# Rows of two tokens: probabilities loaded in the layout of their use, reordered keys sent behind weight piece 3, state copied instead of zeroed, zeroing late

## The chip, the cores and the metric

One core of one Trainium2 chip runs the kernel. The metric is the device time of one execution in microseconds (us). Before the change seven runs lie between 300.64 and 303.35 us, with a median of 302.35 us.

## The reference

```python
f = sigmoid(f_logit)                       # q, k, v, f_logit: [B=4, H=8, S=768, D=48]
for t in range(S):
    state = f[:, :, t, :, None] * state + k_t (x) v_t      # state: [B, H, D, D]
    y[:, :, t] = q_t . state
x = y in rows of tokens                    # [B*S = 3072, H*D = 384]
p = domain_probs / (domain_probs.sum(-1) + 1e-9)           # [3072, E = 4]
out = sum over e of p[:, e] * (relu(x @ w1[e]) @ w2[e])    # w1: 384 x 1024, w2: 1024 x 384
```

A gated linear attention feeds four experts, whose outputs are added with normalised probabilities per token. Probabilities, weights and inputs come from memory as 32-bit numbers; the matrix products are in bf16.

## The kernel before

**Tiling.** The sequence is cut into C = 6 chunks of T = 128 tokens. A chunk has four batches of 8 heads, so its experts work on 4 x 128 = 512 tokens. For a chunk c the attention takes cumulated gates (`cs`, a product with a triangular matrix), exponentials of them, the products q and k with these, their transposes (`tp`), scores (`at`) with a triangular mask, the output `y`, its transpose `xt` into `xT`, and the update of the state (`kv`, `ev_kv`, `state`). The experts take `h` (L476, w1), `relu` (L487 on ScalarE, L485 on VectorE), `o` (L491, w2) and `ev_o` (L498, L500, L502), where the probability of the token is the scalar. VectorE does every `ev_o` with e > 0.

**Chunk 0** has a form of its own: a row holds two tokens, and a tile of 128 rows holds 64 rows of each of two batches. Its products `q` and `k` are in that layout. For its state update (`kv 0.g`, L414) the keys are needed in rows of one batch, so they are sent once more through DMA: `dma_kc` (L371) sends eight copies of 64 KB, from tile `qk` to tile `kc`, on SyncE's queue.

**Who sets the order.** All steps are entered into a planner (`Plan`) with costs, priorities, buffers taken and lags. It plays them through once, and what it gives out is a fixed order of instructions on each engine. SyncE (SP) issues the loads, `dma_kc`, the stores and the DMA transposes in one queue; GpSimd (POOL) issues the loads of v of chunk 0 and eleven weight pieces, which are cast on the way; ScalarE (ACT) issues three early loads. Weight pieces w0 to w3 are halves of w1 for experts 0 and 1, w4 and w5 are halves of w2 for expert 0, and then come whole matrices: w6 is w1 of expert 2, w7 is w2 of expert 1, w8 is w1 of expert 3, w9 is w2 of expert 2, w10 is w2 of expert 3. `after` adds a wait of one transfer for another (f of chunk 1 waits for w6, its second part for w8). Expert products of chunk 0 and steps of attention 1 lie interleaved on TensorE (PE), in the planner's order. PSUM has four buffers `ps_m` for the experts and four `ps_t` for attention. Matmuls on a tile `busy` (L814) fill TensorE ahead of the first expert product where the planner saw a hole.

**At the start** GpSimd builds masks, zeroes pads, then Sf (the 32-bit state, L182) and two tiles Sb (the bf16 state, L186), and only then issues v. VectorE makes `par`, `parb` (L167, a cast of 128 x 2 numbers), `Ui` (L170), `Us` (L173) and masks, among them `mask01` (L180), which attention from chunk 1 on uses.

**Probabilities** are loaded as 24 rows of 2 KB (L277), copied once into the order of two tokens (L283), and turned by eight 32-bit transposes on TensorE (L287, L289) into a `ps_m` buffer. Four VectorE steps (L292 to L295) make `pn` from it.

Of the kernel before, what the change touches and what calls it, by code (L numbers as in the profile page):

```python
# [8 lines left out]
FP32 = mybir.dt.float32  # L9
BF16 = mybir.dt.bfloat16  # L10
# [15 lines left out]
class Plan:  # L26
# [32 lines left out]
    def run(self):  # L59
        for o in self.ops:  # L60
            for k in o.frees:
                self.left[k] = self.left.get(k, 0) + 1
        for o in self.ops:
            if o.name.split(" ")[-1].startswith("0.") and set(o.costs) & {"ACT", "DVE"}:
                o.lag += 0.1
        left = sorted(self.ops, key=lambda o: o.prio)
        free_at = {e: 0.0 for o in left for e in o.costs}
        free_at.update({"DMA": 0.8, "DVE": 5.4, "POOL": 4.6, "ACT": 0.7, "PE": 2.0})
        freeing, done, now = [], [], 0.0
        while left:  # L70
# [33 lines left out]
def kernel(  # L104
# [11 lines left out]
    nc = tc.nc  # L116
# [62 lines left out]
    mask01 = const.tile([T, NP * T], FP32)  # L179
    nc.vector.tensor_copy(out=mask01.rearrange("s (i t) -> s i t", i=NP), in_=U.unsqueeze(1).broadcast_to([T, NP, T]))  # L180
    Sf = const.tile([MP, B, NP, D], FP32)
    nc.gpsimd.memset(Sf, 0.0)  # L182
    Sb = []
    for i in range(2):
        t = const.tile([MP, B, NP, 2 * D], BF16, name=f"sb{i}")
        nc.gpsimd.memset(t, 0.0)  # L186
        Sb.append(t)
    NR = B * C
    praw = const.tile([NR, T, E], FP32)
    ident32 = const.tile([NR, 32], FP32, name="ident32")[:, 0:NR]  # L190
    nc.vector.tensor_copy(out=ident32, in_=ident[0:NR, 0:NR])
    pn = const.tile([T, 2, E, NR], FP32)
    psm = const.tile([T, 2, NR], FP32, name="psm")
    v0 = [const.tile([T, H, 2, D], BF16, name=f"v0{g}") for g in range(2)]
# [8 lines left out]
    for nm, a in (("f", f_logit), ("q", q), ("k", k), ("v", v)):  # L203
# [9 lines left out]
        "cs": ([T, 512], FP32), "tp": ([128, 2, NP, T], BF16), "A": ([T, NP, T], FP32), "y": ([T, 512], FP32),  # L213
        "KV": ([T, 512], FP32), "xp": ([T, KD, T], BF16), "hp": ([128, NT], FP32), "op": ([128, 512], FP32), "pp": ([T, 2, E, NR], FP32),
        "y0": ([T, 512], FP32), "A0": ([T, NP, T], FP32),
    }

    def tl(kind, *key):

        if (kind, key) not in tiles:  # L220
            room = kind if kind in rooms else "ps_m" if kind in ("hp", "op", "pp", "y0", "A0") else "ps_t"
            slot = P.slot[(room, kind) + key if room.startswith("ps_") else (room,) + key]
            if room in ("gp", "qk", "e"):
                tiles[kind, key] = pads[room, slot]
            else:
                shape, dt = shapes[kind]
                pool = ps if room.startswith("ps_") else wk
                tiles[kind, key] = pool.tile(shape, dt, name=f"{room}{slot}")
        return tiles[kind, key]
# [45 lines left out]

    def load_p():
        nc.sync.dma_start(out=praw, in_=moe_domain_probs.rearrange("(r p) e -> r p e", p=T))  # L277

    def praw0():
        return tl("v", 0, 0)[0:NR].rearrange("t h d -> t (h d)")[:, 0:T * E]  # L280

    def p_by_j(eng):
        copy(eng, praw0().rearrange("r (j p e) -> r j p e", j=2, e=E), praw.rearrange("r (p j) e -> r j p e", j=2))  # L283

    def pe_pp():
        for e in range(E):
            nc.tensor.transpose(out=tl("pp")[:, 0, e], in_=praw[:, :, e], identity=ident32)  # L287
        for e in range(E):
            nc.tensor.transpose(out=tl("pp")[:, 1, e], in_=praw0()[:, e::E], identity=ident32)  # L289

    def probs():
        nc.vector.tensor_reduce(out=psm, in_=tl("pp").rearrange("p a e r -> p a r e"), axis=mybir.AxisListType.X, op=ALU.add)  # L292
        nc.vector.tensor_single_scalar(out=psm, in_=psm, scalar=1e-9, op=ALU.add)
        nc.vector.reciprocal(out=psm, in_=psm)
        nc.vector.tensor_tensor(out=pn, in0=tl("pp"), in1=psm.unsqueeze(2).broadcast_to([T, 2, E, NR]), op=ALU.mult)  # L295

# [71 lines left out]
    def dma_kc(n):  # L368
        k = tl("qk", 0, n)[:, 1].rearrange("(p b) h d -> b p (h d)", b=2)
        for b in range(2):  # L370
            nc.sync.dma_start(out=kc[n // 2][b * P2:(b + 1) * P2, n % 2].rearrange("p h d -> p (h d)"), in_=k[b])  # L371

# [77 lines left out]

    def ev_kv(c, b):
        KV = tl("KV", c, b)[:, 0:HD].rearrange("m (i r d) -> m i r d", r=2, d=D)
        for r in range(2):
            rows = slice(r * P2, r * P2 + D)
            nc.vector.tensor_tensor(out=Sf[rows, b], in0=Sf[rows, b], in1=KV[rows, :, r, :], op=ALU.add)  # L455

# [37 lines left out]
    def ev_o(c, e, nt, part, cols, eng):  # L494
        op, o = tl("op", c, e, nt, part)[:, cols], tl("o", c, nt)[:, cols]
        pe = pn[:, 0 if c else 1, e, nt * C + c:nt * C + c + 1]
        if e > 0:
# [69 lines left out]
    def attention0(slot):  # L567
# [3 lines left out]
        def on(f, *x):  # L571
            return lambda e: f(*x)
# [5 lines left out]
        for n in range(B):  # L578
# [13 lines left out]
                       takes=[("qk", 0, n)], frees=[("q", 0, g), ("e", 0, n)])  # L592
            kcd[n] = P.add(f"kc 0.{n}", {"DMA": 0.4}, on(dma_kc, n), -453 + n, deps=[km, wd[2, 1][0]], frees=[("qk", 0, n)], lag=2.0)
            tk = P.add(f"tpk 0.{n}", {"PE": 0.4}, on(pe_tp, 0, n, 1), s(4), deps=[km], takes=[pt_("tp")], frees=[("qk", 0, n)], lag=0.05)
# [18 lines left out]
        for g in range(2):  # L613
# [4 lines left out]
            for b in bs:  # L618
                ek = P.add(f"ev_kv 0.{b}", {"DVE": 0.74}, on(ev_kv, 0, b), s15 + 0.1, deps=[kv], frees=[("ps_t", "KV", 0, b)])
                kvdone[0, b] = P.add(f"state 0.{b}", {"POOL": 1.75}, on(state, 0, b), s15 + 0.2, deps=[ek])  # L620
# [3 lines left out]
    def attention(c, slot, gran):  # L624
# [51 lines left out]
        for b in range(B):  # L676
# [3 lines left out]
            at, vb = AT_[b], VB[b]  # L680
            eA = [P.add(f"ev_at{r} {c}.{b}", {"DVE": 0.7 if c else 0.62}, on(ev_at, r), s(7) + 0.1 + 0.1 * r, deps=[at],
                        takes=[("AT", c, b)], frees=[pt_("A", r)]) for r in range(2)]
# [48 lines left out]
    def add_o(c, e, nt, half):  # L731
# [9 lines left out]
        if half == 1 or by_cols:  # L741
            w = 0.36 if by_cols else 0.62
            ev = oev[c, e, nt] = P.add(f"ev_o {c}.{e}.{nt}.{part}", {"ACT": 0.58, "DVE": 0.56} if e == 0 else {"DVE": w},
                                       lambda g: ev_o(c, e, nt, part, cols, g), p - 1,
                                       deps=[m, oev.get((c, e - 1, nt)), pdone], takes=[("o", c, nt)], frees=[key])
            if e == E - 1:
                P.add(f"store {c}.{nt}.{part}", {"DMA": 0.6}, lambda _: store(c, nt, cols), p - 25, deps=[ev], frees=[("o", c, nt)])

    attention0(lambda n, s: -200 + 14 * (n // 2) + (n % 2) + s * 0.8)
    pl = P.add("ld p", {"DMA": 0.2}, lambda e: load_p(), -989.5, lag=3.0)  # L750
    pj = P.add("p by j", {"POOL": 0.8, "DVE": 0.6}, lambda e: p_by_j(e), -1.5, deps=[pl] + xdone[0, B - 1], takes=[("v", 0, 0)])
    pp = P.add("pp", {"PE": 0.6}, lambda e: pe_pp(), -1, deps=[pj], takes=[("ps_m", "pp")], lag=0.2, frees=[("v", 0, 0)])
    pdone = P.add("probs", {"DVE": 0.9}, lambda e: probs(), 4, deps=[pp] + xdone[0, B - 1], frees=[("ps_m", "pp")])
    ALL, LO, HI = list(range(B)), [0, 1], [2, 3]

# [93 lines left out]
```

## Time and profile before

| | |
|---|---|
| the profiled execution | 301.53 us |
| its span, first to last instruction | 299.8 us |
| granted TensorE clock | 1.000 |
| median of seven runs | 302.35 us |
| TensorE busy | 289.6 us, 97% of the span |
| VectorE, ScalarE, GpSimd busy | 134.0, 172.6, 107.9 us |
| DMA | 36.95 MB in 128974 packets, 118812 of them under 512 B |
| kc, issue to landing | 2.8 to 11.9 us, median 10.3 |
| weight pieces of 384 KB and of 768 KB, issue to landing | median 8.5 and 16.3 us |

All times are us from the span's start. "PEld" is the loading of weights into TensorE, "SPq" and "POOLq" are the queues in which SyncE and GpSimd issue. A row of the timeline gives start, duration, engine, line, operation, output and input, and in brackets the idle time before it with what ended it. A row of the waits gives the waiting engine and line, what it waited for, and the total, the number and the longest. The chain is followed back from the last instruction, so its rows show what set the end.

### The profile page before, as it was taken

The numbers are of one execution on the slowest core, as the hardware profiler recorded it, in microseconds if no ns is written. First come the engines' busy times: TensorE is split into PE (matmuls) and PEld (weight loads), VectorE is DVE, ScalarE is ACT, GpSimd is POOL, SyncE is SP. The second block draws the span as 40 slices with busy tenths as digits, with TensorE's granted clock in tenths as the row PEclk, the third lists the DMA queues.
The fourth block names the chain that finished last, engine by engine and source line by source line (L and its number), as shares of the span: only waits on it lengthen the run. The fifth ranks groups of instructions, "written<-read, shape, count | busy, mean of one in ns | idle before, by whom it ended". The sixth has DMA issues, their size and how long they took to land.

```text
span 299.8 us, 5811 instructions
## 1 busy us (share of the span) xinstructions
PE 289.6 (97%) x2261; PEld 173.8 (58%) x2261; DVE 134.0 (45%) x265; ACT 172.6 (58%) x323; POOL 107.9 (36%) x181
## 2 busy tenths in 40 slices
PE   5899979999999999999999999999999999999995
PEld 2668635567767776455555555555555555555553
DVE  8775115985754675027273353433442322201223
ACT  4875535765665676676477575554465544475440
POOL 8570005847388259124638553235220000000000
PEclk9999999999999999999999999999999999999999
DMA  7999999975979989999799932102331100200002
GB/s 199 213 199 208 205 198 227 191 131 121 192 157 199 183 156 180 230 209 178 133 177 205 194 64 35 28 0 61 95 85 37 26 0 28 77 1 2 0 0 105
DMA packets 128974, 36.95 MB, mean 123 GB/s; under 512 B 118812, under 2 KB 128156, under 8 KB 128948
## 3 DMA queue, kind: packets, MB, share of 16 engines
q1 hardware_dynamic: 118164, 29.29, 49.1%
q0 software_dynamic: 9200, 6.72, 15.3%
q10 hardware_dynamic: 1584, 0.59, 0.8%
q8 instruction: 17, 0.28, 0.4%
q14 instruction: 9, 0.07, 0.1%
HBM read 31.51 MB, written 4.72 MB: 121 GB/s over the span
## 4 chain that ended last, share of the span: by engine, by line
PE 82%; DMA 7%; SPq 3%; ACT 3%; POOL 2%; DVE 1%; issue 1%; POOLq 0%; ACTq 0%
PE ps_m L476 37%; PE ps_m L491 36%; DMA kc<-qk 4%; DMA f<-in_f_logit_dram 3%; PE ps_t L422 2%; SPq L260 2%; PE ps_t L442 1%; POOL qk L352 1%; PE ps_t L438 1%; SPq L374 1%; PE ps_t L310 1%; ACT ex L298 1%; PE ps_t L361 1%; ACT gp L305 1%; PE ps_t L448 1%
## 5 line engine op out<-in xcount | busy, mean ns | idle before, releaser
L476 PE MATMUL ps_m<-xT,w_sb 128*128 128x512 bf16 (+1 forms) x720 | 154.7, 337 | 0.1
L487 ACT ACTIVATE h<-ps_m 128x512 bf16<-128x512 f32 (+1 forms) x188 | 98.5, 527 | 96.5 <-PE ps_m L476 94.2
L491 PE MATMUL ps_m<-w_sb,h 128*128 128x384 bf16 (+1 forms) x776 | 153.8, 324 | 0.0
L491 PEld LDWEIGHTS <-h 128*128 128x128 bf16 x776 | 75.1, 98 | 58.7
L498 DVE SCALAR_TENSOR_TENSOR o<-ps_m,pn,o 128x384 f32<-128x384 f32 (+1 forms) x73 | 44.6, 611 | 107.0 <-PE ps_m L491 99.1
L476 PEld LDWEIGHTS <-w_sb 128*128 128x128 bf16 x720 | 67.8, 98 | 41.2 <-issue 0.3
L485 DVE TENSOR_SCALAR h<-ps_m 128x256 bf16<-128x256 f32 (+1 forms) x52 | 26.1, 510 | 22.2 <-PE ps_m L476 19.8
L462 POOL TENSOR_TENSOR Sf<-Sf,egs 48x192 f32<-48x192 f32 x40 | 21.1, 527 | 37.5 <-DVE Sf L455 35.6
L352 POOL TENSOR_TENSOR qk<-q,e 128x384 bf16<-128x384 f32 x18 | 21.4, 1194 | 27.9 <-ACT e L335 25.5
L335 ACT ACTIVATE e<-ps_t 128x384 f32<-128x384 f32 x48 | 26.7, 667 | 3.2 <-PE ps_t L310 2.1
L431 DVE TENSOR_TENSOR AT<-ps_t,mask 128x512 bf16<-128x512 f32 x40 | 25.0, 683 | 4.7 <-PE ps_t L422 4.7
L455 DVE TENSOR_TENSOR Sf<-Sf,ps_t 48x192 f32<-48x192 f32 x40 | 14.0, 350 | 13.1 <-PE ps_t L448 9.6
L246 POOL CAST vb<-v 128x384 bf16<-128x384 f32 x17 | 8.4, 501 | 31.7 <-issue 14.7
L352 POOL TENSOR_TENSOR qk<-k,e 128x384 bf16<-128x384 f32 x18 | 17.9, 1000 | 4.8 <-DMA k<-in_k_dram 4.6
L463 POOL CAST sb<-Sf 48x192 bf16<-48x192 f32 x40 | 14.1, 352 | 2.6
L500 ACT ACTIVATE o<-ps_m,pn 128x384 f32<-128x384 f32 x22 | 12.8, 581 | 2.8 <-PE ps_m L491 2.0
L298 ACT ACTIVATE ex<-f 128x768 f32<-128x768 f32 (+1 forms) x14 | 10.5, 749 | 5.0 <-DMA f<-in_f_logit_dram 5.0
L342 POOL DMA_DIRECT2D egs<-e x16 | 9.1, 567 | 7.5 <-ACT e L335 7.5
L244 ACT CAST yb<-ps_t 128x384 bf16<-128x384 f32 x17 | 8.1, 477 | 6.2 <-PE ps_t L442 6.2
L305 ACT ACTIVATE gp<-ex 128x768 bf16<-128x768 f32 (+1 forms) x14 | 10.5, 753 | 0.3
L442 PE MATMUL ps_t<-vb,AT 128*128 128x48 bf16 x160 | 10.0, 185 | 0.0
L269 POOL DMA_DIRECT2D w_sb<-in_moe_w_dram x11 | 8.8, 811 | 3.1 <-DMA k<-in_k_dram 2.6
(81 smaller groups left out, 141.0 us busy)
## 6 DMA issues: line engine op xcount, KB each, us to landing
w_sb<-in_moe_w_dram POOLq DMA_DIRECT2D x5, 768.0 KB, 16.3
k<-in_k_dram SPq DMA_DIRECT2D x10, 384.0 KB, 5.2
q<-in_q_dram SPq DMA_DIRECT2D x10, 384.0 KB, 5.2
v<-in_v_dram SPq DMA_DIRECT2D x10, 384.0 KB, 5.6
out_dram<-o SPq DMA_DIRECT2D x19, 192.0 KB, 2.1
f<-in_f_logit_dram SPq DMA_DIRECT2D x9, 384.0 KB, 5.8
w_sb<-in_moe_w_dram POOLq DMA_DIRECT2D x6, 384.0 KB, 8.5
f<-in_f_logit_dram SPq DMA_DIRECT2D x5, 192.0 KB, 5.1
```

The source lines that it names most:

```text
L298: nc.scalar.activation(out=tl("ex", c, b)[:, 0:n * H], in_=tl("f", c, b // 2)[:, hh(b, n), :], func=AF.Exp, scale=-1.0)
L335: nc.scalar.activation(out=o, in_=i, func=AF.Exp, scale=1.0 if j else -1.0)
L352: engines[eng].tensor_tensor(out=tl("qk", c, b)[:, j, :, 0:D].rearrange("t (i r) d -> t i r d", r=2), in0=tl("qk"[j], c, b // 2)[:, hh(b), ...
L431: nc.vector.tensor_tensor(out=tl("AT", c, b)[:, r].rearrange("s i t -> s (i t)"), in0=tl("A", c, b, r).rearrange("s i t -> s (i t)"), in1= ...
L455: nc.vector.tensor_tensor(out=Sf[rows, b], in0=Sf[rows, b], in1=KV[rows, :, r, :], op=ALU.add)
L462: nc.gpsimd.tensor_tensor(out=Sf[rows, b], in0=Sf[rows, b], in1=eg, op=ALU.mult)
L463: nc.gpsimd.tensor_copy(out=nb[rows, b, :, r * D:(r + 1) * D], in_=Sf[rows, b])
L476: nc.tensor.matmul(out=hp(c, e, fc, n0, n1, nf)[:, f], lhsT=w1_sb[:, e, kk, (fc + f) * 128:(fc + f + 1) * 128], rhs=tl("xT", c)[:, kk, n0: ...
L485: nc.vector.tensor_relu(out=dst, in_=src)
L487: nc.scalar.activation(out=dst, in_=src, func=AF.Relu)
L491: nc.tensor.matmul(out=tl("op", c, e, nt, part)[:, cols], lhsT=tl("h", c, e, half_of(c, nt * T))[:, fc, nt * T:(nt + 1) * T], rhs=w2_sb[:, ...
L498: nc.vector.scalar_tensor_tensor(out=o, in0=op, scalar=pe, in1=o, op0=ALU.mult, op1=ALU.add)
```

## The change

Probabilities are no longer transposed. `load_p0` fetches those of chunk 0 in rows of two tokens (two DMAs, 64 x 4 x 4 numbers each) and `load_p1` all of them in rows of one token (one DMA, 128 x 24 x 4 numbers); each piece that lies together is 4 numbers, 16 bytes. They are normalised in place on VectorE, chunk 0 first. The keys' copies wait for w3, and stand ahead of the load of f of chunk 1 in SyncE's queue; `load_p1` waits for w5. Sf is written by a copy in chunk 0, on VectorE or ScalarE. The Sb tiles are zeroed after the tenth weight issue. `mask01` is made after the first normalisation.

```diff
-        free_at.update({"DMA": 0.8, "DVE": 5.4, "POOL": 4.6, "ACT": 0.7, "PE": 2.0})
+        free_at.update({"DMA": 0.8, "DVE": 5.0, "POOL": 4.6, "ACT": 0.7, "PE": 2.0})
...
-    nc.vector.tensor_copy(out=mask01.rearrange("s (i t) -> s i t", i=NP), in_=U.unsqueeze(1).broadcast_to([T, NP, T]))
     Sf = const.tile([MP, B, NP, D], FP32)
-    nc.gpsimd.memset(Sf, 0.0)
     Sb = []
     for i in range(2):
         t = const.tile([MP, B, NP, 2 * D], BF16, name=f"sb{i}")
-        nc.gpsimd.memset(t, 0.0)
         Sb.append(t)
...
-    nc.vector.tensor_copy(out=ident32, in_=ident[0:NR, 0:NR])
...
-    def load_p():
-        nc.sync.dma_start(out=praw, in_=moe_domain_probs.rearrange("(r p) e -> r p e", p=T))
...
-    def pe_pp():
...
+    def load_p0():
+        for j in range(2):
+            nc.sync.dma_start(out=pr0[j * P2:(j + 1) * P2], in_=moe_domain_probs.rearrange("(b c p j) e -> c j p b e", c=C, p=P2, j=2)[0, j])
+
+    def load_p1():
+        after(nc.sync.dma_start(out=pr, in_=moe_domain_probs.rearrange("(r t) e -> t r e", t=T)), ins["w", 5])
+
+    def probs(t, n):
+        m = psm[:, 0:n]
+        nc.vector.tensor_reduce(out=m, in_=t, axis=mybir.AxisListType.X, op=ALU.add)
+        nc.vector.tensor_single_scalar(out=m, in_=m, scalar=1e-9, op=ALU.add)
+        nc.vector.reciprocal(out=m, in_=m)
+        nc.vector.tensor_tensor(out=t, in0=t, in1=m.unsqueeze(2).broadcast_to([T, n, E]), op=ALU.mult)
...
-            nc.sync.dma_start(out=kc[n // 2][b * P2:(b + 1) * P2, n % 2].rearrange("p h d -> p (h d)"), in_=k[b])
+            i = nc.sync.dma_start(out=kc[n // 2][b * P2:(b + 1) * P2, n % 2].rearrange("p h d -> p (h d)"), in_=k[b])
+            after(i, ins["w", 3])
...
-    def ev_kv(c, b):
+    def ev_kv(c, b, eng="DVE"):
...
-            nc.vector.tensor_tensor(out=Sf[rows, b], in0=Sf[rows, b], in1=KV[rows, :, r, :], op=ALU.add)
+            if c == 0:
+                copy(eng, Sf[rows, b], KV[rows, :, r, :])
+            else:
+                nc.vector.tensor_tensor(out=Sf[rows, b], in0=Sf[rows, b], in1=KV[rows, :, r, :], op=ALU.add)
...
-            kcd[n] = P.add(f"kc 0.{n}", {"DMA": 0.4}, on(dma_kc, n), -453 + n, deps=[km, wd[2, 1][0]], frees=[("qk", 0, n)], lag=2.0)
+            kcd[n] = P.add(f"kc 0.{n}", {"DMA": 0.4}, on(dma_kc, n), -456.5 + 0.1 * n, deps=[km, wd[1, 1][1]], frees=[("qk", 0, n)], lag=13.0)
...
-                ek = P.add(f"ev_kv 0.{b}", {"DVE": 0.74}, on(ev_kv, 0, b), s15 + 0.1, deps=[kv], frees=[("ps_t", "KV", 0, b)])
+                ek = P.add(f"ev_kv 0.{b}", {"DVE": 0.6, "ACT": 0.7}, lambda e, b=b: ev_kv(0, b, e), s15 + 0.1, deps=[kv], frees=[("ps_t", "KV", 0, b)])
...
+    def zero():
+        for t in Sb[1], Sb[0]:
+            nc.gpsimd.memset(t, 0.0)
...
+    hi = xdone[0, B - 1]
+    zeroed = P.add("zero", {"POOL": 2.8}, lambda e: zero(), -572.5, deps=[issued[-2]])
+    pl = [P.add("ld p0", {"DMA": 0.3}, lambda e: load_p0(), -970, lag=2.5), P.add("ld p1", {"DMA": 1.0}, lambda e: load_p1(), -454.8, deps=wd[0, 2][1:], lag=14.0)]
+    pdone = [P.add("probs0", {"DVE": 0.9}, lambda e: probs(pr0, B), 4, deps=[pl[0], zeroed] + hi),
+             P.add("probs1", {"DVE": 1.1}, lambda e: probs(pr, NR), 35, deps=[pl[1]])]
+    masked = P.add("mask01", {"DVE": 0.45}, lambda e: mask_later(), 5, deps=[zeroed] + hi)
+    for o in P.ops:
+        if o.name.startswith("state 0."):
+            o.deps.append(zeroed)
```

The scores' evictions (`ev_at`) wait for `masked` in the plan, and `ev_o` takes `pr0` in chunk 0 and `pr` after it.

In the order that results, TensorE has no transposes of probabilities, and otherwise the same instructions up to the first `o`, the filling matmuls included. Call a piece three `h` matmuls of 512 columns or four `o` matmuls. Before, the first `kv 0.g` stands on TensorE behind four pieces of `h` of expert 2 and four of `o` of expert 1; after, behind three and none, and the first `o` of expert 1 follows it. The second stands behind eight and eight pieces before, and behind six and six after. The first step of attention 1 (`cs 1.0`, L310) stands behind three more pieces than before. VectorE's second normalisation (`probs1`) stands between the last `ev_kv 0` and the last `ev_o` of expert 1 in chunk 0. Two of the four `ev_kv 0` are on ScalarE.

More of the change, by code (lines that the diff above doesn't have):

```diff
@@ L185 @@
         t = const.tile([MP, B, NP, 2 * D], BF16, name=f"sb{i}")
-        nc.gpsimd.memset(t, 0.0)
         Sb.append(t)
     NR = B * C
-    praw = const.tile([NR, T, E], FP32)
-    ident32 = const.tile([NR, 32], FP32, name="ident32")[:, 0:NR]
-    nc.vector.tensor_copy(out=ident32, in_=ident[0:NR, 0:NR])
-    pn = const.tile([T, 2, E, NR], FP32)
-    psm = const.tile([T, 2, NR], FP32, name="psm")
+    pr, pr0 = const.tile([T, NR, E], FP32, name="pr"), const.tile([T, B, E], FP32, name="pr0")
+    psm = const.tile([T, 32], FP32, name="psm")
     v0 = [const.tile([T, H, 2, D], BF16, name=f"v0{g}") for g in range(2)]
@@ L213 @@
         "cs": ([T, 512], FP32), "tp": ([128, 2, NP, T], BF16), "A": ([T, NP, T], FP32), "y": ([T, 512], FP32),
-        "KV": ([T, 512], FP32), "xp": ([T, KD, T], BF16), "hp": ([128, NT], FP32), "op": ([128, 512], FP32), "pp": ([T, 2, E, NR], FP32),
+        "KV": ([T, 512], FP32), "xp": ([T, KD, T], BF16), "hp": ([128, NT], FP32), "op": ([128, 512], FP32),
         "y0": ([T, 512], FP32), "A0": ([T, NP, T], FP32),
@@ L220, in tl @@
         if (kind, key) not in tiles:
-            room = kind if kind in rooms else "ps_m" if kind in ("hp", "op", "pp", "y0", "A0") else "ps_t"
+            room = kind if kind in rooms else "ps_m" if kind in ("hp", "op", "y0", "A0") else "ps_t"
             slot = P.slot[(room, kind) + key if room.startswith("ps_") else (room,) + key]
@@ L273, in load_w @@
             after(ins["w", i], ins[1, "k", 0])
-    def load_p():
-        nc.sync.dma_start(out=praw, in_=moe_domain_probs.rearrange("(r p) e -> r p e", p=T))
[L279 to L283, printed above, removed]
-    def pe_pp():
[L286 to L295, printed above, removed]
+    def load_p0():
[9 more added lines that the diff above has]
+        nc.vector.tensor_tensor(out=t, in0=t, in1=m.unsqueeze(2).broadcast_to([T, n, E]), op=ALU.mult)
     def gate1(c, b, n):
@@ L495, in ev_o @@
         op, o = tl("op", c, e, nt, part)[:, cols], tl("o", c, nt)[:, cols]
-        pe = pn[:, 0 if c else 1, e, nt * C + c:nt * C + c + 1]
+        pe = pr[:, nt * C + c, e:e + 1] if c else pr0[:, nt, e:e + 1]
         if e > 0:
@@ L680, in attention @@
             at, vb = AT_[b], VB[b]
-            eA = [P.add(f"ev_at{r} {c}.{b}", {"DVE": 0.7 if c else 0.62}, on(ev_at, r), s(7) + 0.1 + 0.1 * r, deps=[at],
+            eA = [P.add(f"ev_at{r} {c}.{b}", {"DVE": 0.7 if c else 0.62}, on(ev_at, r), s(7) + 0.1 + 0.1 * r, deps=[at, masked],
                         takes=[("AT", c, b)], frees=[pt_("A", r)]) for r in range(2)]
@@ L744, in add_o @@
                                        lambda g: ev_o(c, e, nt, part, cols, g), p - 1,
-                                       deps=[m, oev.get((c, e - 1, nt)), pdone], takes=[("o", c, nt)], frees=[key])
+                                       deps=[m, oev.get((c, e - 1, nt)), pdone[min(c, 1)]], takes=[("o", c, nt)], frees=[key])
             if e == E - 1:
@@ L749, with mask_later @@
     attention0(lambda n, s: -200 + 14 * (n // 2) + (n % 2) + s * 0.8)
[L750 to L753, printed above, removed]
+    def zero():
+        for t in Sb[1], Sb[0]:
+            nc.gpsimd.memset(t, 0.0)
+    def mask_later():
+        nc.vector.tensor_copy(out=mask01.rearrange("s (i t) -> s i t", i=NP), in_=U.unsqueeze(1).broadcast_to([T, NP, T]))
+    hi = xdone[0, B - 1]
[7 more added lines that the diff above has]
+            o.deps.append(zeroed)
     ALL, LO, HI = list(range(B)), [0, 1], [2, 3]
```

## The prediction

> **What bounds the kernel now.** I began with the page's first part: busy time by engine.
>
> ```profile
> PE 289.6 (97%) x2261; PEld 173.8 (58%) x2261; DVE 134.0 (45%) x265; ACT 172.6 (58%) x323; POOL 107.9 (36%) x181
> ```
>
> TensorE is the bound, so a change is worth the TensorE time that it removes plus the TensorE idle time that it closes. The table by stage (start:end, sum, then busy time of PE, PEld, DVE, ACT, POOL with instruction counts) says where that idle time lies:
>
> ```profile
> 24.00:30.00 6.00, 5.87 (x50) 4.81 (x49) 2.96 (x8) 3.07 (x9) 0.00 (x0) 1.00 1.20 208
> ...
> 36.00:42.00 6.00, 5.83 (x32) 2.91 (x30) 0.69 (x2) 3.35 (x6) 0.00 (x0) 1.00 1.24 195
> 42.00:48.00 6.00, 4.24 (x33) 2.25 (x34) 2.29 (x6) 1.19 (x2) 2.28 (x6) 1.00 1.04 223
> ...
> 84.00:90.00 6.00, 5.37 (x41) 3.84 (x40) 3.15 (x7) 4.10 (x8) 5.11 (x11) 1.00 0.68 140
> ```
>
> From 18 us until the last products these are the only holes: 1.9 us around 42, 0.63 us at 87. The waits of TensorE name them:
>
> ```profile
> PE ps_t L414 <- DMA kc<-qk: 1.8, 3, 1.4
> ...
> PE ps_t L310 <- ACT gp L305: 0.6, 1, 0.6
> ```
>
> The chain that ended last shows what else is on the path: the probability transposes in the middle of expert work, and the reordered keys.
>
> ```profile
> 5.99 0.92 PE ps_t L314 x4
> ...
> 25.05 0.59 PE ps_m L287 x4
> 25.64 0.50 PE ps_m L289 x4
> ...
> 33.21 11.27 DMA kc<-qk
> ```
>
> Why the first attention product starts as late as 5.99 is seen in the timeline:
>
> ```profile
> 3.13 2.72 DVE L167 CAST parb<-par 128x2 bf16<-128x2 f32 x1
> 3.13 2.70 POOL L186 MEMSET sb<- 112x1536 bf16 x2
> ...
> 3.21 2.72 DVE L170 TENSOR_SCALAR Ui<-U,par 128x64 bf16<-128x64 f32 x2
> ...
> 5.03 0.52 ACT L305 ACTIVATE gp<-ex 128x384 bf16<-128x384 f32 x1
> ```
>
> A cast of two numbers a partition lasts 2.72 us, exactly while GpSimd zeroes Sb. The gates were ready at 5.55, `Ui` at 5.93.
>
> **Part by part.** All against the profiled execution, 301.53 us (span 299.8, 1.73 around it); it lies 0.82 below the median of 302.35, and I take the difference over unchanged.
>
> *Zeroing leaves the start.* TensorE can start at the gates, 5.55 + 0.05 instead of 5.99: 0.39 us. Behind that stands a chain through ScalarE (four copies of QK, 9.78 to 11.82), so it is carried on. Sf's memset, `ident32` (0.16) and `mask01` (0.43) leave VectorE and GpSimd ahead of the first product k at 7.65, which covers more than 0.39. But v's issue, at 5.77 behind the memsets, moves to about 3.9, when f has landed (0.74 + 3.1), and then shares the DMA engines with q, whose parts land at 7.5 to 7.6 now. Product q starts at 8.12 now and would want q by 7.7. Bounds: the whole 0.39, or nothing. ScalarE copies the k half of QK first (0.51), so q may be half a microsecond late. I take **0.3**.
>
> *Zeroing late.* Two memsets (2.70) behind the tenth weight issue, at about 20.9 to 23.6. GpSimd idles there (0.00 in 24 to 30), and its next use is at 37 or later. Here a rule and a row disagree. The cast row says that VectorE stands while GpSimd zeroes: then `relu` and `ev_xt` at 20.8 to 23.5 are late by up to 2.7 and so is TensorE. The Trainium skill (SBUF — State Buffer, "Who interferes with whom") says that only copies, casts and tensor_scalar from SBUF to SBUF in a two-port mode, or two SBUF inputs against GpSimd reads, meet GpSimd. VectorE's work here reads PSUM. While GpSimd multiplied at 15.06 (1.01), VectorE's yb cast from PSUM took 0.55, as elsewhere; but that was no memset, so the row is only near. I take the rule: **0**, bound 2.7 lost. `mask01` and `probs0` come after the memsets, at 24 to 26, where VectorE is busy 2.96 of 6.
>
> *Transposes.* Eight matmuls of 32-bit numbers, 0.59 + 0.50 of the chain: **1.09** gained. The copy L283 (0.41) and the four steps (0.37, 0.20, 0.46, 0.37 in the chain = 1.40) become two smaller sets of four, which other work hides, but for the wait below. The state's two-row additions (0.375 each) become copies, two of four pairs on ScalarE (3.35 of 6 busy): nothing.
>
> *Keys earlier.* w3 landed at 22.6 (issued 14.0, 8.6 on its way). Eight issues of 0.56 follow; the fourth, which ends the first pair, at 24.8. Even at the slowest landing of today, 11.9, it is there at 36.7. TensorE comes to `kv 0.0` at 41.83 today (43.19 less the 1.36 wait). It comes 0.3 + 1.09 = 1.4 earlier and the step stands five pieces of 0.65 earlier: 41.83 - 1.4 - 3.25 = 37.2. So the wait goes: **1.78** (1.36 + 0.26 + 0.16). What is late next? The keys now share the engines with w4 to w6: 512 KB at the 207 GB/s of 20 to 30 us is 2.6 us at most; as 512 packets of 32 ns (below) over 16 engines, 1.0.
>
> w5 (26.9) becomes 27.9 to 29.5 and is wanted at 30.12 - 1.4 = 28.7. w7 (18.45 + 16.3 = 34.75), with the first of p1's packets (about 1.2), becomes 37.0 to 38.6; wanted behind `kv 0.0` at 37.5. Between 0 and 1.1 lost; nearer the packets' count: **-0.3**.
>
> *Probabilities of all tokens.* 3,072 pieces of 16 bytes, 192 on each of 16 DMA engines, in SyncE's queue ahead of f, k, q and v of chunk 1. No row shows such pieces on that queue. The DMA view (packets, MB, share of 16 engines) of 100 to 150, of 30.7 to 42.6 and of 100 to 200:
>
> ```profile
> q1 hardware_dynamic: 42863, 8.93, 97.0%
> ```
>
> ```profile
> q0 software_dynamic: 2012, 2.01, 100.6%
> q1 hardware_dynamic: 1267, 0.39, 21.3%
> ```
>
> ```profile
> q0 software_dynamic: 257, 0.02, 1.2%
> ```
>
> The first is 192-byte pieces alone: 0.970 x 16 x 50 us / 42,863 = 18.1 ns each. The second, f and keys (q1) beside weights (q0): 32 ns each (and only one per 150 ns and engine). The third, `egs`, also 16-byte pieces but on GpSimd's queue and from one partition: 75 ns. So p1 takes 192 x 18 to 32 ns = 3.5 to 6.1 us of every engine, at the egs price 14.4. The Trainium skill (DMA: Bandwidth & Descriptors, measured bandwidth) gives a floor of 10.5 ns per packet, which would make it an estimate of 2.0; it was measured on GpSimd's queue and without weights beside it, so the rows decide. I take 23.5 ns, nearer the lower: the 32 includes keys of 1 KB. That is 4.5 us.
>
> Who waits: the engines are full until f's second part lands (43.20 + 3.1 = 46.3), so it lands at 50.8. Exponential, logarithm (0.83, 0.84) and hand-over make 1.8: `cs 1.0` ready at 52.6. TensorE comes there at 53.30 - 3.17 + three pieces (1.95) = 52.1. So **-0.5**; zero at 18 ns, -2.1 at 32, -10.4 at 75. The other waiter is `probs1` on VectorE, reached at about 45.5; behind it stand the `ev_o` of expert 1 and a `relu`. TensorE ends that expert at 50.09 - 3.17 + 0.45 = 47.4 and has PSUM buffers for five pieces, to 50.6; less 1.40 and 0.62, p1 must be there by 48.5. It is (50.8 less 128 packets of 18 ns), just. It is the same lateness, not added. p0, 512 pieces, is 0.6 us of the engines where k, q load; k and q in return are issued 1.25 sooner, as the old load's slot is gone: 0.
>
> *Gap at 87.* f of chunk 2 (issued 80.52, landing 86.4) stands behind the stores of chunk 0 and two transposes in SyncE's queue, and those wait for work of TensorE that comes 3 us sooner. `cs 2.2` also stands nine `h` matmuls of 0.11 and eight `o` of 0.16 later, 2.3 us. Gap closed: **0.63**; bound 0.
>
> Sum: 0.3 + 1.09 + 1.78 + 0.63 - 0.3 - 0.5 = 3.0. Profiled 298.5; median 302.35 - 3.0 = **299.35**.
>
> **Rivals.** (1) *Same*: p1 at 32 ns (-2.1) and weights at -0.8: 3.8 - 2.9 = 0.9 gained, 301.45. For it: f took 11.9 us beside the weights; against it: 16 bytes are less than 192. (2) *The keys still come late*: were they slowed to 14 us, they would land at 38.8, 1.6 behind TensorE: 1.4 gained, 300.95. Against it: today f's packets stand in front of them, then nothing does. (3) *Slower*: 16-byte pieces cost nearly what egs shows. From 39 ns each (7.5 us, -3.5 at `cs 1.0`) nothing is left of 3.5; midway to 75, at 57 ns, 10.9 us cost 6.9 and the time is 302.35 + 3.4 = 305.75. Place: TensorE idle before `cs 1.0`, f landing past 55. Against it: those packets come from one partition, by another queue.
>
> **Numbers.** Forecast 0.70 (298.4 to 300.6), same 0.13 (300.6 to 302.6), keys late 0.06, slower 0.11. No change that a measurement can tell is within 0.5%, 1.5 us: the forecast, half of the late keys and the near end of the same lie below 300.84, 0.70 + 0.03 + 0.03 = 0.76 faster; the rest of these two, 0.13, is within it; slower 0.11. The range, 297.9 to 302.4, leaves out the slower rival and a little at each end; below the best sum (302.35 - 3.9 = 298.4) it allows 0.5 for the scatter of seven runs.
>
> **What would show it.** Right: no row of L287 or L289, the parb cast under 0.2 us, first cs at 5.6, no wait of TensorE for kc, f's second part at 49 to 51, the expert products dense from 18 us. Wrong: VectorE rows of 1 us or more at 21 to 24; TensorE waiting for weights at 37; VectorE waiting for p1 past 48.5 or ScalarE for f past 51; a new gap of TensorE before the first product of chunk 1.

## The result and the profile after

The changed kernel takes **298.8 us** (median of 12 runs, 298.03 to 300.73) against 302.38 (31 runs): a ratio of **0.9894**, 95% interval 0.9872 to 0.9916. The forecast was 299.35 in 297.9 to 302.4. Run again later among the experiments, on another chip, it took 300.68 (7 runs) against 302.48, 0.9929 [0.9901, 0.9958]. The ratios are taken over the executions in the fast state and are not the quotients of the medians shown. The profiled execution took 298.79 us with a span of 297.0; both are 2.7 us less than before.

The page's first part: TensorE has the eight transposes less, and VectorE 3.9 us less.

```profile
PE 287.8 (97%) x2253; PEld 172.6 (58%) x2253; DVE 130.1 (44%) x264; ACT 173.5 (58%) x326; POOL 107.3 (36%) x180
```

The table by stage, columns as before (stretch, sum, busy time of PE, PEld, DVE, ACT, POOL, granted clock, DMA share, GB/s):

```profile
24.00:30.00 6.00, 6.00 (x52) 4.81 (x50) 2.69 (x10) 4.10 (x11) 0.00 (x0) 1.00 1.18 220
36.00:42.00 6.00, 6.00 (x48) 3.25 (x47) 1.95 (x4) 3.20 (x7) 3.36 (x8) 1.00 1.42 204
42.00:48.00 6.00, 6.00 (x47) 3.13 (x45) 2.84 (x8) 3.22 (x8) 3.29 (x8) 1.00 1.12 182
54.00:60.00 6.00, 5.34 (x52) 3.11 (x52) 4.88 (x9) 3.11 (x6) 2.21 (x2) 1.00 1.10 186
84.00:90.00 6.00, 5.40 (x42) 3.83 (x40) 3.00 (x7) 4.42 (x8) 4.93 (x11) 1.00 0.82 163
```

The hole of 1.9 us around 42 is gone, the one of 0.6 at 87 is still there, and a new one of 0.66 lies in 54 to 60. TensorE's waits name both:

```profile
PE ps_m L482 <- DMA w_sb<-in_moe_w_dram: 0.7, 1, 0.7
PE ps_t L297 <- ACT gp L292: 0.6, 1, 0.6
```

The timeline at the start and at the new place of the zeroing:

```profile
3.13 0.17 DVE L167 CAST parb<-par 128x2 bf16<-128x2 f32 x1
3.21 0.42 DVE L170 TENSOR_SCALAR Ui<-U,par 128x64 bf16<-128x64 f32 x2
...
20.52 2.71 POOL L743 MEMSET sb<- 112x1536 bf16 x2
20.95 0.56 DVE L240 CAST yb<-ps_t 128x384 bf16<-128x384 f32 x1 [0.21 <-PE ps_t L394]
21.72 0.42 DVE L476 TENSOR_SCALAR h<-ps_m 128x256 bf16<-128x256 f32 x1 [0.21 <-PE ps_m L467]
```

The cast takes 0.17 instead of 2.72. Beside the same memset, VectorE's steps that read PSUM last as long as elsewhere (0.56, 0.42), as the rule said that the prediction took, and the cast's row did not.

The chain that ended last no longer holds transposes or keys. It runs through transfers:

```profile
31.61 9.57 SPq L254
...
41.27 2.79 SPq L254
...
44.11 4.30 DMA k<-in_k_dram
...
48.94 10.11 DMA w_sb<-in_moe_w_dram
59.05 0.05 issue
59.09 0.82 PE ps_m L482 x4
...
78.71 6.50 DMA f<-in_f_logit_dram
...
86.11 0.85 ACT gp L292
...
87.00 0.48 PE ps_t L297 x2
```

SyncE's two issues of f of chunk 1 take 9.57 and 2.79 us behind the probabilities' pieces; the k of chunk 1 follows, and the last weight piece (call it w10) may only be issued when that k has landed, at 48.4. So it lands at 59.05, and `o` of expert 3 waits.

**Where the time went.** For this I took the start of the same expert product in both traces, at places where the numbers of `h`, of `o` and of attention products done before it are the same. What the changed kernel is ahead by (differences taken before rounding):

| the next expert product | before, us | after, us | ahead |
|---|---|---|---|
| the first of all | 17.55 | 17.12 | 0.43 |
| behind weight piece w3 | 23.25 | 23.09 | 0.16 |
| behind the transposes' place | 26.05 | 24.74 | 1.32 |
| twelve products on | 27.67 | 26.05 | 1.62 |
| behind the first keys (16 `kv` products done in both) | 44.79 | 40.59 | 4.20 |
| behind the wait for w10 | 68.68 | 65.20 | 3.48 |
| the last of all | 296.38 | 292.88 | 3.49 |

The keys' step can be read from each trace alone, too. Between four `o` and the next `h`, TensorE makes 16 `kv` products. Before, at the first keys:

```profile
41.01 0.81 PE L491 MATMUL ps_m<-w_sb,h 128*128 128x384 bf16 x4
43.19 0.21 PE L414 MATMUL ps_t<-v,kc 64*128 64x96 bf16 x1 [1.36 <-DMA kc<-qk]
43.66 0.34 PE L414 MATMUL ps_t<-v,kc 64*128 64x96 bf16 x7 [0.26 <-DMA kc<-qk]
44.15 0.21 PE L414 MATMUL ps_t<-v,kc 64*128 64x96 bf16 x1
44.52 0.34 PE L414 MATMUL ps_t<-v,kc 64*128 64x96 bf16 x7 [0.16 <-DMA kc<-qk]
44.79 0.82 PE L476 MATMUL ps_m<-xT,w_sb 128*128 128x512 bf16 x3
```

After, at the second keys, where nothing waits:

```profile
42.54 0.81 PE L482 MATMUL ps_m<-w_sb,h 128*128 128x384 bf16 x4
43.28 0.51 PE L402 MATMUL ps_t<-v,kc 64*128 64x96 bf16 x16
43.73 0.82 PE L467 MATMUL ps_m<-xT,w_sb 128*128 128x512 bf16 x3
```

From the first `o` to the `h` it is 3.78 us before and 1.19 after: 2.59 less, where the table has 2.58 (4.20 less 1.62).

From the start of the last product to the end of the span it is 4.13 us after and 3.37 before, 0.76 more, which leaves 2.7 of the 3.5. In all nine profiles of kernels with the whole change it is 4.07 to 4.14. The last store is issued 3.40 us ahead of the end, where it was 2.64 before; SyncE's waits for the stores stand between. Why they take longer was not tested.

### The profile page after: what moved, and what is told of

The parts are those of the page before. It is cut to its first block, busy times and chain, and to the rows that moved or that the text cites. A ratio compares the mean times of both kernels' runs of the same rounds, so it can differ in the third digit from the quotient of the medians.

```text
span 297.0 us, 5789 instructions
## 1 busy us (share of the span) xinstructions
PE 287.8 (97%) x2253; PEld 172.6 (58%) x2253; DVE 130.1 (44%) x264; ACT 173.5 (58%) x326; POOL 107.3 (36%) x180
## 4 chain that ended last, share of the span: by engine, by line
PE 71%; DMA 14%; SPq 7%; POOL 4%; issue 2%; ACT 1%; DVE 0%; POOLq 0%
PE ps_m L482 34%; PE ps_m L467 32%; DMA w_sb<-in_moe_w_dram 8%; SPq L254 6%; DMA k<-in_k_dram 3%; DMA f<-in_f_logit_dram 2%; PE ps_t L410 2%; POOL w_sb L263 1%; SPq L252 1%; PE ps_t L430 1%; POOL qk L339 1%; PE ps_t L426 1%; PE ps_t L297 1%; PE ps_t L436 1%; SPq L362 0%
## 5 line engine op out<-in xcount | busy, mean ns | idle before, releaser
L478 ACT ACTIVATE h<-ps_m 128x512 bf16<-128x512 f32 (+1 forms) x192 | 100.2, 527 | 92.1 <-PE ps_m L467 88.3
L489 DVE SCALAR_TENSOR_TENSOR o<-ps_m,pr,o 128x384 f32<-128x384 f32 (+1 forms) x73 | 44.6, 612 | 93.4 <-PE ps_m L482 87.0
L476 DVE TENSOR_SCALAR h<-ps_m 128x256 bf16<-128x256 f32 (+1 forms) x48 | 24.0, 507 | 27.1 <-PE ps_m L467 24.9
L453 POOL TENSOR_TENSOR Sf<-Sf,egs 48x192 f32<-48x192 f32 x40 | 20.1, 502 | 32.5 <-DVE Sf L240 14.6
L240 POOL CAST vb<-v 128x384 bf16<-128x384 f32 x17 | 9.8, 582 | 29.9 <-PE ps_t L436 22.4
L446 DVE TENSOR_TENSOR Sf<-Sf,ps_t 48x192 f32<-48x192 f32 x32 | 11.2, 350 | 10.6 <-PE ps_t L436 10.1
L491 ACT ACTIVATE o<-ps_m,pr 128x384 f32<-128x384 f32 x22 | 12.8, 581 | 3.6 <-PE ps_m L482 2.8
L426 PE MATMUL ps_t<-sb,QK 112*128 112x96 bf16 x80 | 9.9, 204 | 0.0
```

The source lines that it names most:

```text
L453: nc.gpsimd.tensor_tensor(out=Sf[rows, b], in0=Sf[rows, b], in1=eg, op=ALU.mult)
L476: nc.vector.tensor_relu(out=dst, in_=src)
L478: nc.scalar.activation(out=dst, in_=src, func=AF.Relu)
L489: nc.vector.scalar_tensor_tensor(out=o, in0=op, scalar=pe, in1=o, op0=ALU.mult, op1=ALU.add)
```

## The experiments

First the parts of the change one by one on the kernel before, then the start, the pieces of 16 bytes and the two waits that are left. The experiments' ratios are to the kernel before, run beside them: 302.75, 302.48 and 301.66 us in the three groups.

### Late zeroing alone

```diff
-    nc.gpsimd.memset(Sf, 0.0)
...
-        nc.gpsimd.memset(t, 0.0)
...
+    zeroed = P.add("zero", {"POOL": 3.5}, lambda e: zero(), -572.5, deps=[issued[-2]])
```

> The kernel before with one part of the change alone: the states are zeroed behind the issue of the tenth weight piece instead of at the start. Theory A (what is gained ahead of the keys is swallowed, because the keys of the first chunk land at a time that the transfers set): the first expert product stands 0.3 to 0.45 us sooner, the wait for the keys grows by as much, and the time stays at 302.4 (within 0.2). Rival B (the gains add, as the prediction summed them): 0.3 to 0.4 less, 302.0 to 302.1.

Measured: 304.01 us, ratio **1.0042** [1.0020, 1.0065]. Slower: both theories missed. The chain from the start of its trace, and its stretch of 12 to 14 us:

```profile
4.51 6.94 DMA k<-in_k_dram
11.45 0.28 issue
11.73 0.76 POOL w_sb L267
...
13.87 7.82 DMA w_sb<-in_moe_w_dram
21.69 0.05 issue
21.73 1.16 PE ps_m L474 x9
```

```profile
12.00:14.00 2.00, 1.79 (x50) 1.61 (x49) 1.67 (x4) 1.97 (x6) 2.00 (x4) 1.00 0.31 28
```

Without the memsets GpSimd issues v at 4.2 instead of 5.8, before SyncE issues the k of batch 2 (4.5). That k lands at 11.4 instead of 9.7, the first weight piece is held until it has, and from 12 to 14 the engines move 28 GB/s where they moved 152. TensorE waits 1.4 us for the second weight piece and is 2.3 us behind at 25 us; even the first expert product comes 0.4 later, not sooner. The keys are not a fixed mark either: they hang on the weights' queue and land 2.2 later too. So theory C, made from this result: **the memsets at the start were a useful delay of v.**

### Putting v back, two ways

The changed kernel with v waiting for the first k, and the changed kernel with the zeroing at the start again:

```diff
-    v_gate, w_hold, issued = {0: (0, "f", 1)}, {0: (0, "k", 2), 1: (0, "q", 2)}, []
+    v_gate, w_hold, issued = {0: (0, "k", 0)}, {0: (0, "k", 2), 1: (0, "q", 2)}, []
```

> The changed kernel with one wait moved: the first v is issued when the first k of chunk 0 has landed (about 6.3 us), not when the second f has (4.0), so it goes about when it went in the kernel before. Theory C (without the zeroing at the start, v's transfer goes in front of the k that holds the first weight piece, and every weight piece comes later by it): the first weight piece is issued at 9.7 to 10.1 instead of the 10.28 and 11.34 of the two profiles of the changed kernel, the stretch of 12 to 14 us moves 150 GB/s or more again, and the time is 0.985 to 0.990 of before. Rival (v is what the start waits for): the products of v come 2 us later, and the time stays at 0.990 to 0.994.

```diff
+    nc.gpsimd.memset(Sf, 0.0)
...
+        nc.gpsimd.memset(t, 0.0)
...
-    zeroed = P.add("zero", {"POOL": 2.8}, lambda e: zero(), -572.5, deps=[issued[-2]])
```

> The changed kernel with one part undone: the states are zeroed at the start again, on the same engine and place as in the kernel before. Theory C: the first weight piece is issued at 9.7 to 10.1, the cast of parb takes 2.7 us again, the first gate product comes 0.4 later, and the time is that of the changed kernel or up to 0.4% less: 0.986 to 0.990 of before. Rival, the prediction's step (late zeroing is worth 0.3 us): 0.3 us or 0.1% more than the changed kernel, 0.991 to 0.994.

The changed kernel itself, profiled a second time:

> The changed kernel itself, as the mark for the kernels that go with it on the same chip: 298.8 (298.4 to 299.2). Its profile shows once more the two waits that the change leaves: 0.7 us for the last weight piece at 59 and 0.6 us for the gates at 87.

Measured: v behind k 298.79, 0.9879 [0.9834, 0.9925]; zeroing at the start 298.69, 0.9873 [0.9824, 0.9921]; the changed kernel again 300.68, 0.9929 [0.9901, 0.9958]. The last missed what was expected of it (298.8), which had been taken from another chip; the expectations in us of the other kernels that were set from it are off likewise, and their ratios are to be read. The intervals overlap, so the times lean to theory C and don't prove it; the traces show the mechanism, that v ahead of the k delays the first weight piece. GpSimd's timeline with v behind k:

```profile
6.20 1.58 POOL L246 DMA_DIRECT2D v<-in_v_dram  x2 [3.68 <-DMA k<-in_k_dram]
9.16 0.76 POOL L263 DMA_DIRECT2D w_sb<-in_moe_w_dram  x1 [1.39 <-DMA k<-in_k_dram]
```

First weight issue in the fourteen profiled executions: with the zeroing at the start 9.6 to 10.2 (five), with it late 10.28 to 11.73 (seven; 10.28 in the first profile of the changed kernel, 11.34 in its second), with it late and v behind k 9.2 and 9.3, sooner than theory C had said. From 12 to 14 us the engines move 193 GB/s with v behind k, 149 with the zeroing at the start, and 48 in that second profile. Against it, v behind k is 1.40 us ahead at 24 us; with the zeroing at the start it is 1.20. But 1.08 and 0.43 are left at 59, and 0.38 and -0.08 at 87: the waits for w10 and for the gates take the gain. The size depends on the execution that is taken as the mark: against the first profile of the changed kernel, v behind k is 0.02 ahead at 24 us and the zeroing at the start 0.19 behind. Shown is that the late zeroing alone costs time; whether it does within the whole change is not.

### The keys alone

```diff
+            after(i, ins["w", 3])
...
-            kcd[n] = P.add(f"kc 0.{n}", {"DMA": 0.4}, on(dma_kc, n), -453 + n, deps=[km, wd[2, 1][0]], frees=[("qk", 0, n)], lag=2.0)
+            kcd[n] = P.add(f"kc 0.{n}", {"DMA": 0.4}, on(dma_kc, n), -456.5 + 0.1 * n, deps=[km, wd[1, 1][1]], frees=[("qk", 0, n)], lag=13.0)
```

> The kernel before with one part alone: the reordered keys of the first chunk wait for weight piece 3, and so go ahead of the other small transfers. Theory A: the wait for the keys cost TensorE the whole 2.6 us by which its products of the two traces draw apart there; all of it goes, 299.8. Rival B: it cost the 1.78 us of the rows of waits, 300.6. Either way no wait for the keys is left, and the one expert product of chunk 0 that now needs the last weight piece waits for it for up to 0.7, which would put A at 300.5.

Measured: 300.55 us, **0.9923** [0.9892, 0.9954], 2.3 us less (1.4 to 3.3): theory A's 2.6 and B's 1.8 both lie inside. The trace decides for A at that place: TensorE was 0.22 behind from the start and is 2.38 ahead behind the first keys (counted by `o`, as a few `h` are missing from that trace), so the wait had cost 2.6, as in the whole change. No wait for w10 showed. Another one came:

```profile
PE ps_t L423 <- DMA QK<-qk: 1.2, 1, 1.2
```

TensorE now reaches a DMA transpose of attention 1 before it has landed, and its last product ends only 1.1 us sooner than before. The rest of the 2.3 us fits the lowered clock (last section), which the kernel before met more often: without it, the medians are 300.25 us here (6 runs) and 301.98 before (27 runs).

### The probabilities alone, two places for the second part

The direct loads with nothing else; `load_p1` behind weight piece 5 (so ahead of f and of the late keys), or behind v of chunk 1:

```diff
-    pl = P.add("ld p", {"DMA": 0.2}, lambda e: load_p(), -989.5, lag=3.0)
...
+    pl = [P.add("ld p0", {"DMA": 0.3}, lambda e: load_p0(), -970, lag=2.5), P.add("ld p1", {"DMA": 1.0}, lambda e: load_p1(), -454.8, deps=wd[0, 2][1:], lag=14.0)]
```

> The kernel before with one part alone: the probabilities are loaded directly, the second part behind the issue of weight piece 5, and no transpose of them is left; the keys stay late. Theory A: the second part's 3072 small pieces now stand ahead of f and of the late keys, so these land later, and the 1.1 to 1.5 us that TensorE gains at the transposes are lost again at the keys with more beside: 302.4 to 304.5, with a longer wait for the keys. Rival B (the pieces cost little and the gains add): 301.3.

> As the kernel with the direct loads alone, but the second part of the probabilities is loaded only behind the v of chunk 1, so nothing new stands ahead of the keys. Theory A: TensorE comes 1.1 to 1.5 us sooner to the keys, which land when they landed before; the wait grows by that, and the time stays at 302.4 (within 0.3). Rival B: the 1.1 us come through, 301.3.

Measured: 305.25 us, 1.0052 [1.0020, 1.0085] with the pieces ahead, 302.43 us, 0.9983 [0.9961, 1.0004] with them behind. The times are theory A's, the first even longer than it said, but its path shows only in the first. In the second, TensorE is 1.29 ahead at 27.7 and the keys are where they were (11.27 before):

```profile
33.21 11.07 DMA kc<-qk
```

Still the wait for them doesn't grow (1.8 before):

```profile
PE ps_t L404 <- DMA kc<-qk: 1.7, 4, 1.0
```

In the planner's new order one more piece of `h` and one of `o` stand ahead of the first `kv`, so the lead is kept as work done. It goes behind the keys: in this execution TensorE's clock is halved for 3.4 us from 44.0 on (last section), which costs at most 1.7 us by that length, and TensorE is 0.04 ahead from 48 to 54 us. Then it waits 0.8 for w10, and the last product comes 1.2 later than before. Among executions without a lowered clock, the medians are 301.80 us (11 runs) and 301.98 before (27), so there the gain doesn't come through either; where it is lost in them no trace shows.

With the pieces ahead, the keys are issued from 39.1 to 46.4 instead of 31.2 to 42.6, and the wait grows from 1.8 to 2.7:

```profile
PE ps_t L404 <- DMA kc<-qk: 2.7, 3, 2.0
```

The wait for w10 is 1.5 there, and this execution has the halved clock behind the keys as well, so its loss isn't that of the pieces alone.

### Twice the pieces of 16 bytes

```diff
+    prx = const.tile([T, NR, E], FP32, name="prx")
...
+        for t in pr, prx:
+            after(nc.sync.dma_start(out=t, in_=moe_domain_probs.rearrange("(r t) e -> t r e", t=T)), ins["w", 5])
```

> The changed kernel, but the probabilities of all tokens are loaded a second time, into a tile that nothing reads, directly behind the first. If such pieces cost the engines their own time (20 ns each, 192 on each engine: 3.8 us), f, k and with it the last weight piece land 3 to 4 us later, the wait for that piece grows from 0.7 to 3 or 4, and the time is 3 us above the changed kernel, 1.000 to 1.004 of before. If they are nearly free beside the weights: f lands at most 1 us later, and the time at most 1 us above, 0.990 to 0.996.

Measured: 302.86 us, 1.0017 [0.9979, 1.0055]: the first theory's time, but not by its path. Beside the second profile of the changed kernel (whose first load of the probabilities is issued at the same 30.5), k of chunk 1 is issued 46.31 instead of 45.36, only 1.0 later, w10 also 1.0 later, but `o` gets it 2.0 later (61.71 and 59.75):

```profile
PE ps_m L484 <- DMA w_sb<-in_moe_w_dram: 2.4, 1, 2.4
```

At the gates of chunk 2 it is 2.8 behind, at the end 3.5. Per extra piece and engine (192 of them) that is 5 ns at k and 10 ns at w10, less than the 23.5 ns of the prediction; the rest is added at the later waits. Of the 14 runs 9 had a lowered clock (last section); the other five have a median of 301.34 us.

### The two waits that are left

w10 issued behind the second f; f of chunk 2 loaded ahead of its k, q, v; both; both with v behind the first k:

```diff
-            after(ins["w", i], ins[1, "k", 0])
+            after(ins["w", i], ins[1, "f", 1])
...
-                    add_load(c + 2, nm, 2 * half, 2, u0 + {0: 38}.get(c, 30) + 4 * half + j, deps=wd[3, 1])
+                    add_load(c + 2, nm, 2 * half, 2, u0 + {0: 38}.get(c, 30) + (0.5 if (c, half, nm) == (0, 1, "f") else 4 * half + j), deps=wd[3, 1])
```

> The changed kernel, but the last weight piece is issued when the second part of f has landed, not when the first k of chunk 1 has. Theory A (the piece is late only because its issue hangs on k): it lands 1.5 to 2 us sooner, the 0.7 us wait goes and shows in the time: 298.1. Rival: its bytes then stand ahead of k and q of chunk 1, whose readers wait instead, or the later wait for the gates takes the gain: 298.8 or more.

> The changed kernel, but the f of chunk 2 is loaded ahead of k, q and v of that chunk. Theory A (the gap at 87 is that load's queue and nothing else): f lands some 2 to 4 us sooner, the 0.6 us gap goes: 298.2. Rival: the k of chunk 2 comes later and its products wait instead: 298.8 or more.

> The changed kernel with both: the last weight piece issued on f, and the f of chunk 2 loaded first. If both waits are on the chain of the end and nothing is late behind them: 297.5 (298.8 less 0.7 less 0.6). If one gain is taken by the other place or by the stores at the end: 298.1 to 298.8.

> The changed kernel with three waits moved: v behind the first k, the last weight piece issued on f, the f of chunk 2 loaded ahead of its k, q and v. Theory C with the gains adding: 0.3% below the kernel with the last two alone, 0.985 to 0.987 of before, 297.8 to 298.4. If the start is covered by a later wait (the keys, the last weight piece, the gates at 87): 0.989, as without it.

| kernel | us | ratio to before | interval |
|---|---|---|---|
| changed, again | 300.68 | 0.9929 | 0.9901 to 0.9958 |
| w10 sooner | 300.48 | 0.9931 | 0.9899 to 0.9962 |
| f of chunk 2 sooner | 299.80 | 0.9917 | 0.9885 to 0.9948 |
| both | 299.24 | 0.9889 | 0.9863 to 0.9915 |
| both, v behind k | 298.52 | 0.9863 | 0.9818 to 0.9909 |

The last row was measured beside 301.66 us, the others beside 302.48. One alone gives nothing that can be told.

With w10 sooner its wait goes, and against the first profile of the changed kernel TensorE is 0.46 ahead at 59, but level at 74 (-0.06), and it loses 0.9 at 116. There the first `h` of a chunk waits 0.8 us. The DMA transpose into its `xT` is issued at 112.15 (110.89 in that profile) and such take about 4 us, so this is the likely wait; the profile's rows don't name it.

With f sooner, the gates of chunk 2 are ready at 82.4 instead of 87.2 in the second profile of the changed kernel. But the planner puts their product sooner as well, and TensorE still waits 0.4 there. It is also 1.3 behind that profile at 76, because it waits 0.9 for the first part of the gates of chunk 2. Both waits are in this row:

```profile
PE ps_t L297 <- ACT gp L292: 1.3, 2, 0.9
```

The f of the first part is issued at 70.1 instead of 68.4, behind stores whose six issues take 5.2 us instead of 3.7; why they do stays open.

The waits of TensorE with all three moved:

```profile
PE ps_t L301 <- ACT gp L292: 1.6, 2, 1.4
PE ps_m L817 <- DVE busy L145: 1.5, 1, 1.5
PE ps_t L297 <- DVE AT L419: 0.6, 1, 0.6
PE ps_m L379 <- ACT QK L238: 0.2, 1, 0.2
```

No weight is among them. The wait of 0.6 is that of the gates' product of chunk 2, at 79.08: its row names VectorE's masked scores (`AT`) because those ended last, but the gates were ready only about 0.04 us before them, at 79.02. Against the first profile of the changed kernel TensorE is 0.9 us ahead at 17, 1.7 at 59 and 1.6 at the last product, so here what the start gained is not taken later. This execution, with a span of 295.4, is the fastest of its six runs (297.24 us). The kernel has the lowest ratio of all here, though its interval overlaps those of the changed kernel.

## Why the prediction was right, and where it was wrong

The sign and the size hold, 3.0 predicted and 2.7 of span or 3.6 of the medians measured. That the sum came so near is in part luck: several terms were wrong and offset each other, the 0.76 us behind the last product was no term, and the medians hold a lowered clock before (last section) that the prediction didn't know of.

| step | predicted | measured |
|---|---|---|
| zeroing leaves the start | 0.3 | 0.43, then 0.16 at w3; alone -1.3 of the whole time |
| zeroing late | 0 | 0 |
| transposes | 1.09 | 1.16, and 0.3 at the buffer they held |
| the wait for the keys | 1.78 | 2.6 |
| weight pieces | -0.3 at w7 | -0.27 at w3 (in the start's row), none at w7, -0.72 at w10 |
| second part of the probabilities | -0.5 at `cs 1.0` | 0 there, part of the -0.72 at w10 |
| gap at 87 | 0.63 | 0.03 |
| behind the last product | no term | -0.76 |

- **Start.** "Bounds: the whole 0.39, or nothing" was the failed sentence. It looked at v against q, and not at what else lies behind v's earlier transfer: the k that holds the first weight piece. The bound should have gone below nothing; the run with this part alone shows 0.4% lost. In the first profile of the changed kernel the weights came only 0.26 later (10.28 against 10.02), so little showed.
- **Late zeroing.** Right, and the page's rule that the prediction took decided rightly over the cast's row: no VectorE step from 20.5 to 23.2 grew.
- **Transposes.** Right in size for TensorE's own part. The four VectorE steps that held the `ps_m` buffer were called hidden, but the last of them set the start of an expert product before:

```profile
27.26 0.37 DVE pn L295
27.63 0.04 issue
27.67 1.47 PE ps_m L476 x12
```

  The 0.3 is inferred from the two traces, not tested alone. How much of the 1.16 and the 0.3 counts without the early keys is not shown: with the late pieces, in one trace the lead is gone at 48 us, but behind a halved clock.
- **Keys.** Mechanism right, the term undersized: TensorE was said to come at 41.83 and `kv` to cost nothing but its waits of 1.78. The waits' rows count only the gaps in front of scattered products, whose modelled ends fill part of the stall; the whole step from `o` to `h` shrank by 2.6, and with this part alone the products moved by 2.6 too.
- **Second part of the probabilities.** Its pieces were priced at 23.5 ns, and f was to land at 50.8. It landed at 46.6 (46.3 before); that the keys' transfers had left its way is the likely reason, and the pieces cost less: the doubled load shows about 5 ns each at k and 10 at w10. `cs 1.0` didn't wait. The cost is real, but it shows at w10, a waiter that the prediction didn't list: it is issued only when k has landed. Rivals 1 and 3 fall with that price, rival 2 with the landing of the keys, 6.0 to 6.5 us after their issue.
- **Gap at 87.** "Those wait for work of TensorE that comes 3 us sooner" failed. f of chunk 2 is issued 1.8 sooner (78.71 against 80.52) and lands 1.2 sooner (85.2 against 86.4), and TensorE comes about 1.2 sooner as well. Ahead of the issue stand DMA transposes that wait for GpSimd's products of attention 1, and those stand later in the new order. With f moved in front of k, q and v the gates come 4.6 to 4.9 sooner, which shows that the queue's order is what holds them. The gap itself stays in part (0.4 of 0.6), as the order of the products moves with the gates.
- **Behind the last product.** The prediction had the end unchanged without saying so. The 0.76 us there is in every profile of the whole change, and its cause is open.

What most of this has in common: from 10 to 87 us the kernel has a row of marks set by transfers (weights, keys, w10, gates of chunk 2). A gain ahead of a mark counts only if the mark moves as well, and a transfer that moves to the front can move all marks back.

## What to carry to other kernels

Before removing early idle work on an engine that also issues DMAs, ask which transfer now jumps the queue, and which landing gates the big transfers behind it. Price a wait by the starts of the same products in two traces, or by the gap from arrival to the next product, not by the waits' rows alone. Follow a gain from mark to mark along the transfers: it is worth what is left behind the last of them. A fix that shows nothing alone may only be taken by the next mark: by the times, w10 and f of chunk 2 together lean to a gain that neither has alone, but the intervals overlap and the trace of both shows none.

## What was not expected of the hardware

**A hole of two microseconds can be followed by a halved clock of TensorE.** The stretches (same columns) around the wait for the keys, in the kernel with the late second part of the probabilities:

```profile
42.00:44.00 2.00, 0.62 (x9) 0.36 (x9) 0.00 (x0) 0.00 (x0) 0.00 (x0) 1.00 0.82 221
44.00:46.00 2.00, 1.61 (x10) 0.75 (x12) 1.05 (x4) 0.00 (x0) 0.64 (x2) 0.51 1.04 208
46.00:48.00 2.00, 2.00 (x8) 0.96 (x7) 0.76 (x2) 0.60 (x1) 1.72 (x5) 0.64 1.18 235
48.00:50.00 2.00, 2.00 (x13) 1.12 (x12) 0.22 (x1) 1.09 (x2) 1.01 (x3) 1.00 1.21 227
```

The granted clock is 1.00 until 44 and has means of 0.51 and 0.64 over the next two stretches; if it is half while it is lowered, that makes 3.4 us. The execution with the pieces ahead of the keys shows the same behind its hole. The profile of the kernel before doesn't show it, but of its 88 runs beside the experiments 41 had a mean clock below 0.9965 (3.4 us at half would make it 0.994), and their median was 303.64 us against 301.79 for the other 47.

How often it comes goes with the hole. With the wait for the keys: 41 of 88 before, 16 of 22 with the late zeroing alone, 13 of 15 and 11 of 22 with the pieces ahead and behind. With a hole of 2.4 us at 59, under the doubled load: 9 of 14. Without such a hole: none of 19 with the changed kernel, none with v behind k, with f of chunk 2 sooner, with both waits moved and with all three (25 runs), 2 of 8 with w10 sooner, 1 of 6 with the zeroing at the start, 2 of 8 with the keys alone, where another wait of 1.2 us is left. So it is rarer there, not absent, and and that the hole causes it rests on these counts and two traces; no run varies the hole's length alone.

The Trainium skill (TensorE: Matmul & The Clock Gate, "What's actually happening") says that the clock halves after an idle window of some 3.4 us that runs freely. The free running fits that only about half of the runs are hit, and the length fits the 3.4 us. But here a shorter hole, not even idle throughout, is enough: the last expert product ahead of the keys ends at 41.83, nine small `kv` products follow, and the clock is down from 44.0 on. Closing the hole is then worth, by an estimate from these counts and medians, 41/88 x 1.85 = 0.9 us more on average than in the profile of an execution that was not hit. That fits the 3.6 us of the medians beside 2.7 of span.

**Pieces of 16 bytes pass slowly and delay what follows by less.** The 192 pieces on each engine took 15.4 us from issue to landing, 80 ns each, beside the weights' transfers, whose packets took 97.5% of the engines' time in that stretch; by the doubled load, what waits behind pays 5 to 10 ns for each.
